# A fused attention and MLP block on one core: mixer in four groups of 112 channels, row turns and shared-key copies by DMA, w4 in the place of the q/k/v weights, and a new order

## The chip, the cores and the metric

The kernel runs on one core of one Trainium2 chip. The metric is the device time of one execution in microseconds (us); lower is better. Four engines compute: TensorE (PE, with its weight loads shown apart as PEld), VectorE (DVE), ScalarE (ACT) and GpSimd (POOL). SyncE (SP) only issues DMAs here; every DMA of the kernel is issued from SP, in SP's program order, and each engine runs its own instructions strictly in the order in which the program lists them.

## The reference

One sequence of 2048 positions with 448 channels, bf16. First a sliding local attention with 16 heads of 28 channels, in which a position sees itself and seven earlier positions two apart; then a mixer that shifts four channel groups along the sequence; then an MLP with 1792 hidden channels.

```
def _A_ref(x, wqkv, wo):
    H = 16; Dh = D // H; W, dil = 8, 2
    qkv = (x @ wqkv).reshape(B, S, 3, H, Dh)
...
    idx = pos[:, None] - off[None, :]
    mask = idx >= 0
...
    logits = jnp.einsum("bhsd,bhswd->bhsw", q, kg) * scale
    logits = jnp.where(mask[None, None, :, :], logits, -1e9)
    attn = _softmax(logits, axis=-1)
    o = jnp.einsum("bhsw,bhswd->bhsd", attn, vg)
...
def _B_ref(x, w1, w2, w3, w4):
    h = _gelu(_layernorm(x, axis=-1) @ w1)
    c = D // 4
    g0 = jnp.pad(h[:, :, 0*c:1*c], ((0, 0), (1, 0), (0, 0)))[:, :S, :]
    g1 = jnp.pad(h[:, :, 1*c:2*c], ((0, 0), (0, 1), (0, 0)))[:, 1:, :]
    g2 = jnp.pad(h[:, :, 2*c:3*c], ((0, 0), (2, 0), (0, 0)))[:, :S, :]
    g3 = jnp.pad(h[:, :, 3*c:   ], ((0, 0), (0, 2), (0, 0)))[:, 2:, :]
    hs = jnp.concatenate([g0, g1, g2, g3], axis=-1) @ w2
    x1 = x + hs
    h2 = _gelu(_layernorm(x1, axis=-1) @ w3) @ w4
    return x1 + h2
...
    h = x + _A_ref(_layernorm(x, axis=-1), A_wqkv, A_wo)
    h2 = h + _B_ref(_layernorm(h, axis=-1), B_w1, B_w2, B_w3, B_w4)
```

Here `off` is `arange(W) * dil`, and `kg` and `vg` are k and v at the positions `idx`.

## The kernel before

The sequence is cut into four blocks of 512 rows (t = 0 to 3) for attention and mixer, and into five units (u = 0 to 4) of 2, 4, 4, 4 and 2 tiles of 128 rows for what follows. A phase and its block or unit are written together: A23 is phase A2 of block 3, W30 is phase W3 of unit 0, T0 is phase T of unit 0.

Phases of a block. N1: layer norm of the input (written "N12" for block 2). A1: the normalized rows are turned so that channels lie on partitions, and q and k are formed; the last 64 channels of q and k of all heads go through a pair of banks X and Y into `qT` and `kr`, the other 384 into `qT` and `kk`. The keys of a block need the last 16 positions of the block before; these shared keys are copied between `kk[t]` and `kk[t+1]`, and between the halves of `kr` (lines 707 to 711), by ACT. V: the values, and SP's DMAs that lay them out in `vw` for each of the eight window positions (`vwp`, `vwa`, `vwb`, `vwc`). A2: DVE multiplies q with eight shifted views of k, in four pieces c (three of 128x4096, the last, from `kr`, of 128x2048), and PE sums over the channels of each head. S: softmax, with the weighting `pb` and a turn by PE. A3: DVE spreads the weights with a mask into `bd_r`, PE multiplies with `vw`, the result is evicted to `actT`. O: the projection with wo and the residual sum. B1: layer norm of the result and a turn by DMA. M: the mixer's first matmul with GELU into `gT`.

Phases of a unit. B2: the mixer's second matmul from the shifted `gT`, DVE adds the residual. T: layer norm and a turn by DMA. W3: the first MLP matmul with GELU into `h3T`. B3: the second one, from which DVE makes the output tiles in a ring of NO buffers that SP stores.

K and N of a matmul of 448 channels are cut into pieces with 64 rows: the helper `duo` (line 459) runs an upper and a lower half of the array side by side on two outputs, first one way round and then the other. Line 482, `sums`, deals the seven 64-channel pieces to them.

In the mixer before, `w1_s` has 512 columns: the 448 channels are put in another sequence and 64 of them appear twice, so that M makes four full groups of 128 columns. Where a group holds channels with different shifts, a second GELU writes part of its rows to another place (`MOVED`, lines 846 to 852). The 448 channels then stand in seven halves of 64 rows, and B2 needs seven matmuls for a tile; a pair of tiles takes 14.

A turn is done by PE (letter 't' in `TURN`: 32 small transposes into PSUM and two evictions for a block) or by one DMA transpose ('d'). Normalization and eviction may be given to ACT or DVE; `OTHER` lists those that leave their first engine, among them two of the four `pb` weightings, which GpSimd makes.

The order is written out by hand: every operation has a number in the sequence in which the phases create it, and `ORDER` lists all 891 numbers. Each engine runs its share of that list; the waits follow from what an operation reads and writes and from when its buffer comes free (`arrange`, line 192). All loads stand in one sequence on SP: x and the q/k/v weights first, then wo, w1 in six pieces, w2 in five, w3, w4. The arena holds w3, the q/k/v weights and w4 side by side.

Of the kernel before, what the change touches and what calls it, by code (L numbers as in the profile page):

```python
# [5 lines left out]
ACT = mybir.ActivationFunctionType  # L6
# [43 lines left out]
"""  # L50
OTHER = """
104 127 196 197 199 402 408 411 519 525 528 582 583
# [79 lines left out]
class _Sched:  # L132
# [59 lines left out]
    def arrange(self, sequence, other=()):  # L192
# [4 lines left out]
        done = set()  # L197
        self.gorder = []
        for n, k in enumerate(sequence):
# [3 lines left out]
            op.deps |= op.sdeps  # L203
            for d in op.deps | op.odeps:
                if d not in done:
                    raise RuntimeError("operation %d (%s) stands before %d (%s)" % (k, op.tag, d.idx, d.tag))
# [68 lines left out]
def bass_sequential_preLN__sliding_local_dilated__mixer_s_mlp__prompt_kernel(  # L275
# [6 lines left out]
    NST = SEQ // 512  # L282
# [12 lines left out]
    SHIFT = {(0, 0): 1, (0, 1): -2, (1, 0): -2, (1, 1): -2, (2, 0): 2, (2, 1): -1, (3, 0): -1, (3, 1): -1}  # L295
    MOVED = {0: (64, 48, 3), 1: (96, 32, 4), 2: (64, 16, 3)}
# [4 lines left out]
    A_W4 = A_W + 4 * (1344 + 128)  # L301
    A_QG = A_W4 + NF * 448
# [6 lines left out]
    with ExitStack() as es:  # L309
# [13 lines left out]
        w1_s = sb("w1_s", [128, 4, 512], BF16)  # L323
# [3 lines left out]
        st6 = sb("st6", [128, 8, 6], F32)  # L327
        mv = sb("mv", [128, 3, NTL, 2], F32)
# [20 lines left out]
        P_h3 = _Pool("h3", lambda k: h3T[:, k, :], NF + 2)  # L349
        P_st = _Pool("st", lambda k: st6[:, k, :], 8)  # L350
# [70 lines left out]
        def load_x(i, n):  # L421
            return dma("x%d" % i, xin[:, i:i + n, :], xv[:, i:i + n, :], 128 * n * D * 2)

        def load_rows(chan, dst, src, lo, n):

            for h in range(2):
                dma("%s%s" % (chan, "ab"[h]), dst[:, 2 * h:2 * h + 2, :], src[192 * h:192 * h + 256, lo:lo + n].rearrange("(c k) n -> k c n", k=128), 256 * n * 2)
# [21 lines left out]
        w4_v = B_w4.rearrange("(f k) n -> k f n", k=128)  # L449
        for f in range(0, NF, 7):  # L450
            dma("w4%d" % f, w4_s[:, f:f + 7, :], w4_v[:, f:f + 7, :], 128 * 7 * D * 2)
        for eng in ("sp", "pool", "act"):
# [576 lines left out]
```

## Time and profile before

| | us |
|---|---|
| timed runs, lowest / median / highest (3) | 192.61 / 193.52 / 194.06 |
| profiled execution | 193.18 |
| its span, first to last instruction | 191.7 |

All instructions appear under line 987, where the list is issued, so groups are told apart by their tiles: `arena` holds weights, q, k, `gT` and residual sums, `ps` is PSUM, `lntm` normalized rows, `actT` turned rows. `ps<-w_s,arena` is B2, `ps<-actT,w_s` M, `ps<-qk_r,zc` A2's sums, `ps<-bd_r,vw` A3, `ps<-ident,lntm` the turns by PE. A group's line has its count, its busy time and the mean time of one instruction in ns. Matmul ends are modelled, and matmuls overlap. In the list of stretches, each engine's busy time within the stretch stands before its number of instructions.

The page in 40 slices, each digit the busy share in tenths, with the granted TensorE clock:

```profile
PE   6999999999999868989999999999999999999994
PEld 2584533453444333347545444455444544555672
DVE  7799999999999999899876960036988022002203
ACT  4579999999999999999594998860148004821340
POOL 3240000000004000202076000022077600000000
PEclk9999999999999999999999999999999999999999
DMA  5999791004604179480805024006100812000111
```

### The profile page before, as it was taken

What the parts mean: (1) busy time and instruction counts of PE and PEld (TensorE: products, weight loads), DVE (VectorE), ACT (ScalarE), POOL (GpSimd) and SP (SyncE); (2) the same over time, 40 slices, a digit from 0 to 9 for tenths busy, and PEclk for the clock granted to TensorE, in tenths of its full rate; (3) what the DMA queues carried; (4) which work ended last, traced back from release to release, by engine and by line L of the source; (5) the groups of instructions that cost most, each with busy time, mean ns of one, the idle gap of its engine ahead of it and who ended that gap; (6) DMA issues with size and microseconds to landing.
All of it is one profiled execution on the core that took longest, in us unless ns stands there. A gap on an engine that the chain in (4) does not pass through costs nothing.

```text
span 191.7 us, 5740 instructions
## 1 busy us (share of the span) xinstructions
PE 181.3 (95%) x2482; PEld 92.6 (48%) x2482; DVE 129.5 (68%) x229; ACT 132.9 (69%) x310; POOL 29.3 (15%) x63
## 2 busy tenths in 40 slices
PE   6999999999999868989999999999999999999994
PEld 2584533453444333347545444455444544555672
DVE  7799999999999999899876960036988022002203
ACT  4579999999999999999594998860148004821340
POOL 3240000000004000202076000022077600000000
PEclk9999999999999999999999999999999999999999
DMA  5999791004604179480805024006100812000111
GB/s 144 349 268 186 190 320 36 10 3 118 149 3 85 28 64 262 140 178 5 109 3 113 2 50 87 0 3 146 36 27 0 164 51 72 0 3 0 51 48 48
DMA packets 30272, 17.03 MB, mean 89 GB/s; under 512 B 18936, under 2 KB 29736, under 8 KB 30248
## 3 DMA queue, kind: packets, MB, share of 16 engines
q1 hardware_dynamic: 30248, 16.68, 36.7%
q8 instruction: 19, 0.31, 0.7%
q14 instruction: 5, 0.04, 0.1%
HBM read 8.04 MB, written 1.84 MB: 51 GB/s over the span
## 4 chain that ended last, share of the span: by engine, by line
PE 66%; ACT 21%; DVE 5%; DMA 2%; POOL 1%; issue 1%; SPq 1%; POOLq 0%; ACTq 0%
PE ps L987 66%; ACT arena L987 7%; ACT lntm L987 4%; ACT actT L987 2%; DMA vw<-vt 2%; ACT vt L987 2%; ACT L982 1%; DVE lntm L987 1%; DVE st L987 1%; SPq L987 1%; ACT xin L987 1%; ACT ls L987 1%; ACT L987 1%; DVE bd_r L987 1%; DVE actT L987 1%
## 5 line engine op out<-in xcount | busy, mean ns | idle before, releaser
L987 PE MATMUL ps<-actT,arena 64*128 64x256 bf16 (+1 forms) x756 | 68.8, 329 | 1.3 <-DVE arena L987 0.7
L987 ACT ACTIVATE h3T<-ps 128x512 bf16<-128x512 f32 (+1 forms) x70 | 30.3, 525 | 39.3 <-PE ps L987 39.2
L987 PEld LDWEIGHTS ps<-actT,arena 64*128 64x128 bf16 x756 | 35.5, 94 | 30.7 <-PE ps L987 2.1
L987 PE MATMUL ps<-arena,h3T 64*128 64x448 bf16 (+2 forms) x434 | 44.4, 344 | 0.0
L987 ACT ACTIVATE arena<-ps 128x512 bf16<-128x512 f32 (+10 forms) x86 | 40.1, 515 | 3.5 <-PE ps L987 2.8
L987 DVE SCALAR_TENSOR_TENSOR ost<-ps,mrs,arena 128x448 bf16<-128x448 f32 (+1 forms) x17 | 10.6, 652 | 36.4 <-PE ps L987 36.4
L987 DVE TENSOR_TENSOR qk_r<-arena 128x4096 bf16<-128x4096 bf16 (+1 forms) x16 | 32.0, 2017 | 0.7 <-PE ps L987 0.5
L987 PEld LDWEIGHTS ps<-arena,h3T 64*128 64x128 bf16 (+1 forms) x434 | 23.0, 94 | 18.7 <-issue 0.2
L987 POOL TENSOR_TENSOR arena<-arena,xin 128x448 f32<-128x448 f32 x16 | 17.2, 1091 | 45.3 <-DVE lntm L987 45.3
L987 DVE TENSOR_TENSOR bd_r<-arena,bmask 80x2048 bf16<-80x2048 bf16 x16 | 18.9, 1213 | 0.9 <-PE ps L987 0.7
L987 ACT ACTIVATE actT<-ps 128x512 bf16<-128x512 f32 (+2 forms) x21 | 14.6, 743 | 2.1 <-PE ps L987 2.1
L987 PE MATMUL ps<-wo_s,actT 64*128 64x448 bf16 x128 | 14.3, 351 | 0.6 <-DVE actT L987 0.4
L987 PE MATMUL ps<-actT,w_s 64*128 64x512 bf16 x112 | 13.3, 377 | 1.5 <-ACT rs_y L987 0.7
L987 PE MATMUL ps<-arena,actT 64*128 64x448 bf16 x112 | 12.4, 350 | 0.4 <-ACT vt L987 0.4
L987 PE MATMUL ps<-w_s,arena 64*128 64x448 bf16 x112 | 11.6, 350 | 0.9 <-ACT arena L987 0.7
L987 ACT ACTIVATE lntm<-xin,nm 128x448 bf16<-128x448 bf16 x16 | 10.5, 661 | 2.6 <-DVE nm L987 2.6
L987 DVE SCALAR_TENSOR_TENSOR arena<-xin,rs_y,ps 128x448 f32<-128x448 bf16 x16 | 10.3, 672 | 2.1 <-PE ps L987 2.0
L987 DVE TENSOR_SCALAR lntm<-arena,mv,rs_y 128x512 bf16<-128x512 f32 x14 | 10.2, 774 | 2.1 <-POOL rs_y L987 2.0
L987 POOL TENSOR_TENSOR pb<-ls,mx 128x512 bf16<-128x512 f32 x2 | 3.3, 1640 | 52.6 <-ACT mx L987 52.6
L987 DVE BATCH_NORM_STATS2 st<-xin 128x6 f32<-128x448 bf16 x16 | 9.4, 614 | 0.8 <-DMA xin<-in_A_x_dram 0.8
L987 PEld LDWEIGHTS ps<-actT,w_s 64*128 64x128 bf16 x112 | 5.2, 94 | 8.6 <-PE ps L987 1.7
L987 PEld LDWEIGHTS ps<-wo_s,actT 64*128 64x128 bf16 x128 | 5.6, 94 | 7.2 <-PE ps L987 1.4
(73 smaller groups left out, 161.9 us busy)
## 6 DMA issues: line engine op xcount, KB each, us to landing
arena<-in_B_w_dram SPq DMA_DIRECT2D x2, 896.0 KB, 6.7
out_dram<-ost SPq DMA_DIRECT2D x15, 112.0 KB, 1.8
arena<-in_B_w_dram SPq DMA_DIRECT2D x2, 784.0 KB, 5.7
vw<-vt SPq DMA_DIRECT2D x4, 320.0 KB, 4.3
vw<-vt SPq DMA_DIRECT2D x4, 256.0 KB, 4.3
arena<-in_A_wqkv_dram SPq DMA_DIRECT2D x2, 448.0 KB, 5.0
xin<-in_A_x_dram SPq DMA_DIRECT2D x2, 448.0 KB, 7.5
xin<-in_A_x_dram SPq DMA_DIRECT2D x3, 224.0 KB, 5.6
```

What stands on the lines that cost most here:

```text
L982: eng.preload_act_table_set("natural_log_exp_and_others")
L987: inst = getattr(eng, meth)(**kw)
```

## The change

The mixer's groups become the reference's own four of 112 channels: `w1_s` and `w2_s` have 448 columns and 112 rows in use, each group has one shift, the second GELUs and the clearing after them go, and B2 runs four pieces in each half (64 and 48 rows), 16 matmuls for a pair of tiles. The rows of blocks 2 and 3 are turned for A1 by DMA. The shared keys are copied by DMAs of 16-element runs on SP, four in blocks 0 to 2 and two in block 3. w4 is put where the q/k/v weights lie and loaded after V3. All four `pb` weightings are on DVE. The output ring has five buffers, the loads of w1 and w2 are one of two pieces and one of one. ORDER is new, with 858 numbers; on SP it has the sequence x and q/k/v weights; block 0's shared keys; the turn of A12; V0's value copies mixed with block 1's keys; the turn of A13; wo; V1's copies; further keys, w1 and the turn of B10; w2 and the turn of B11; w3; the turn of T0; V3's copies and w4; the turn of B12. Other engines' shares change with it: on PE, W30 begins before A23's last two sums and the second half of B21; after M3 comes one group of B31 and then B23; on DVE, A23's last two products and two residual adds of O2 stand behind T0's normalizations, two evictions of A32 and one more normalization of B10 go to ACT, and T1's normalizations stand ahead of A33's last masks.

`HALO = 'dddd'` selects the key DMAs. `STAGE = '....'` and `ALONE = False` leave their branches unused.

```
-TURN = {'A1': 'tttt', 'B1': 'dddd', 'B2': 'ddddd'}
+TURN = {'A1': 'ttdd', 'B1': 'dddd', 'B2': 'ddddd'}
-NBD, NLN, NACT, NSM, NO = 3, 2, 4, 1, 3
+NBD, NLN, NACT, NSM, NO = 3, 2, 4, 1, 5
+HALO = 'dddd'
+STAGE = '....'
+ALONE = False
 ORDER = """
...
-    SHIFT = {(0, 0): 1, (0, 1): -2, (1, 0): -2, (1, 1): -2, (2, 0): 2, (2, 1): -1, (3, 0): -1, (3, 1): -1}
-    MOVED = {0: (64, 48, 3), 1: (96, 32, 4), 2: (64, 16, 3)}
+    SHIFT = (-1, 1, -2, 2)
+    GC = D // 4
...
-    A_W4 = A_W + 4 * (1344 + 128)
-    A_QG = A_W4 + NF * 448
+    A_W4 = A_W
+    A_QG = A_W4 + max(NF * 448, 4 * (1344 + 128))
...
-        for k, (to, lo, n) in enumerate(((0, 112, 336), (336, 0, 112), (448, 48, 64))):
-            load_rows("w1%d" % k, w1_s[:, :, to:to + n], B_w1, lo, n)
-        dma("w2", w2_s[:, 0:2, :], B_w2[112:368, :].rearrange("(c k) n -> k c n", k=128), 256 * D * 2)
-        for k, (lo, c, src, n) in enumerate(((0, 2, 368, 80), (80, 2, 0, 48), (0, 3, 48, 64), (64, 3, 48, 64))):
-            dma("w2%d" % k, w2_s[lo:lo + n, c, :], B_w2[src:src + n, :], n * D * 2)
+        load_rows("w1", w1_s, B_w1, 0, D)
+        dma("w2", w2_s[0:GC, :, :], B_w2.rearrange("(c k) n -> k c n", k=GC), D * D * 2)
...
+            if HALO[t] == "d":
...
+                    end = lambda h, lo, n: kr[t][64 * h:64 * h + 64, lo:lo + n, 64:]
+                dma("kra%d" % t, kr[t][64:128, :, 0:PADK], end(0, 0, 4), 64 * 4 * PADK * 2)
+                dma("krb%d" % t, kr[t][0:64, 1:4, 0:PADK], end(1, 0, 3), 64 * 3 * PADK * 2)
+                if t + 1 < NST:
+                    dma("krc%d" % t, kr[t + 1][0:64, 0:1, 0:PADK], end(1, 3, 1), 64 * PADK * 2)
+                    dma("kkc%d" % t, kk[t + 1][:, :, 0:PADK], kk[t][:, :, 512:KVW], 128 * 3 * PADK * 2)
+            else:
...
-            S.add("dve", "tensor_tensor", alts=[("pool", [("tensor_tensor", mult)])], **mult)
+            dve("tensor_tensor", **mult)
...
             def group(g, upper):
                 b = _Tile(P_bank)
-                def evict():
-                    act(gT[:, g, 2 + t * 512:2 + (t + 1) * 512], b(), ACT.Gelu_apprx_tanh)
-                    if g in MOVED:
...
+                return sums(lambda lo, n: b(halves(lambda v: v[0:GC, lo:lo + n], n // 128)), lambda c, part: w1_s[part, c, g * GC:(g + 1) * GC],
+                            lambda c, part, lo, n: rows(a, c, lo // 128, n // 128, part), upper), \
+                    lambda: act(gT[0:GC, g, 2 + t * 512:2 + (t + 1) * 512], b(lambda v: v[0:GC, :]), ACT.Gelu_apprx_tanh)
...
+        def load_w4():
+            last = S.ops[-1]
+            w4_v = B_w4.rearrange("(f k) n -> k f n", k=128)
+            for f in range(0, NF, 7):
+                dma("w4%d" % f, w4_s[:, f:f + 7, :], w4_v[:, f:f + 7, :], 128 * 7 * D * 2).odeps.add(last)
...
-                return (lambda lo, n: b(lambda v: v[:, lo:lo + n]), side(0, 3 + upper), side(1, 4 - upper)), out
+                return (lambda lo, n: b(lambda v: v[:, lo:lo + n]), side(TOP), side(slice(64, GC))), out
...
+                    if S.tag == "V%d" % (NST - 1):
+                        S.tag = "w4"
+                        load_w4()
```

More of the change, by code (lines that the diff above doesn't have):

```diff
@@ L197, in arrange @@
         done = set()
+        turned, moved = [], []
         self.gorder = []
@@ L203, in arrange @@
             op.deps |= op.sdeps
+            if not ALONE:
+                pass
+            elif op.insts[0][0] == "dma_start_transpose":
+                op.deps.update(turned + moved)
+                turned, moved = [op], []
+            elif op.is_dma and not callable(op.chan):
+                op.deps.update(turned)
+                moved.append(op)
             for d in op.deps | op.odeps:
@@ L442, in bass_sequential_preLN__sliding_local_dilated__mixer_s_mlp__prompt_kernel @@
             dma("wo%d" % j, wo_s[32 * j:32 * j + DH, :, :], wo_v[j], DH * D * 8)
[L443 to L455 removed]
+        load_rows("w1", w1_s, B_w1, 0, D)
+        dma("w2", w2_s[0:GC, :, :], B_w2.rearrange("(c k) n -> k c n", k=GC), D * D * 2)
+        load_rows("w3", w3_s, B_w3, 0, F)
+        loads = [op for op in S.ops if op.is_dma]
+        for a, b in zip(loads, loads[1:]):
+            b.odeps.add(a)
         TOP, BOT = slice(0, 64), slice(64, 128)
@@ L703, in phase_A1 @@
             duo(half(X, 0, True), half(Y, 64, False), ((0, 256),))
-            for h, b in enumerate((X, Y)):
-                copy(qT[64 * h:64 * h + 64, 3, now:now + 256], b(lambda v: v[0:64, 0:256]))
-                copy(kr[t][64 * h:64 * h + 64, :, PADK:], b(lambda v: v[64:128, 0:256].rearrange("p (j n) -> p j n", j=4)), False)
-            copy(kr[t][64:128, :, 0:PADK], last(X, 0, 4), False)
-            copy(kr[t][0:64, 1:4, 0:PADK], last(Y, 0, 3), False)
-            if t + 1 < NST:
-                copy(kr[t + 1][0:64, 0:1, 0:PADK], last(Y, 3, 1), False)
-                copy(kk[t + 1][:, :, 0:PADK], kk[t][:, :, 512:KVW])
+            if STAGE[t] == "d":
+                stage = _Tile(P_sg)
+                for h, b in enumerate((X, Y)):
+                    copy(stage(lambda v, h=h: v[:, h, :]), b(lambda v: v[:, 0:256]))
+                for h in range(2):
+                    dma("sq%d%d" % (t, h), qT[64 * h:64 * h + 64, 3, now:now + 256], stage(lambda v, h=h: v[0:64, h, :]), 64 * 512)
+                    dma("sk%d%d" % (t, h), kr[t][64 * h:64 * h + 64, :, PADK:], stage(lambda v, h=h: v[64:128, h, :].rearrange("p (j n) -> p j n", j=4)), 64 * 512)
+            else:
+                for h, b in enumerate((X, Y)):
+                    copy(qT[64 * h:64 * h + 64, 3, now:now + 256], b(lambda v: v[0:64, 0:256]))
+                    copy(kr[t][64 * h:64 * h + 64, :, PADK:], b(lambda v: v[64:128, 0:256].rearrange("p (j n) -> p j n", j=4)), False)
@@ new lines, in phase_A1 @@
+            if HALO[t] == "d":
+                if STAGE[t] == "d":
+                    end = lambda h, lo, n: stage(lambda v: v[64:128, h, :].rearrange("p (j n) -> p j n", j=4)[:, lo:lo + n, 64 - PADK:])
+                else:
+                    end = lambda h, lo, n: kr[t][64 * h:64 * h + 64, lo:lo + n, 64:]
[4 more added lines that the diff above has]
+                    dma("kkc%d" % t, kk[t + 1][:, :, 0:PADK], kk[t][:, :, 512:KVW], 128 * 3 * PADK * 2)
+            else:
+                copy(kr[t][64:128, :, 0:PADK], last(X, 0, 4), False)
+                copy(kr[t][0:64, 1:4, 0:PADK], last(Y, 0, 3), False)
+                if t + 1 < NST:
+                    copy(kr[t + 1][0:64, 0:1, 0:PADK], last(Y, 3, 1), False)
+                    copy(kk[t + 1][:, :, 0:PADK], kk[t][:, :, 512:KVW])
@@ L718, in group @@
                 b = _Tile(P_bank)
-                return sums(lambda lo, n: b(lambda v: v[:, 0:D]), lambda c, part: a(lambda v: v[part, il, c, :]),
-                            lambda c, part, lo, n: wqkv_s[part, c, 2 * D:3 * D], upper), \
+                return sums(lambda lo, n: b(lambda v: v[:, lo:lo + n]), lambda c, part: a(lambda v: v[part, il, c, :]),
+                            lambda c, part, lo, n: wqkv_s[part, c, 2 * D + lo:2 * D + lo + n], upper), \
                     lambda: copy(vt[:, sl, il, :].rearrange("p (h n) -> p h n", n=32)[:, :, 0:DH], b(lambda v: v[:, 0:D].rearrange("p (h n) -> p h n", n=DH)))
@@ L868, in phase_B2, with group, side @@
             summed = STATS["B2"][u] == "a"
-            def group(i, upper):
+            def group(i):
                 b = _Tile(P_bank)
-                def side(h, n):
-                    part = (TOP, BOT)[h]
-                    return [(gT[part, c, 2 + i * 128 + SHIFT[c, h]:130 + i * 128 + SHIFT[c, h]], (lambda lo, m, c=c: w2_s[part, c, lo:lo + m])) for c in range(n)]
+                def side(part):
+                    return [(gT[part, c, 2 + i * 128 + SHIFT[c]:130 + i * 128 + SHIFT[c]], (lambda lo, m, c=c: w2_s[part, c, lo:lo + m])) for c in range(4)]
                 def out():
@@ L910, in group @@
                 b = _Tile(P_bank)
-                return sums(lambda lo, m: b(halves(lambda v: v[:, 0:128 * n], n)), lambda c, part: w3_s[part, c, f * 128:(f + 1) * 128],
-                            lambda c, part, lo, m: rows(a, c, 0, n, part), upper), \
+                return sums(lambda lo, m: b(halves(lambda v: v[:, lo:lo + m], m // 128)), lambda c, part: w3_s[part, c, f * 128:(f + 1) * 128],
+                            lambda c, part, lo, m: rows(a, c, lo // 128, m // 128, part), upper), \
                     lambda: act(h3[u][f](lambda v: v[:, 0:128 * n]), b(lambda v: v[:, 0:128 * n]), ACT.Gelu_apprx_tanh)
```

27 lines of the change are left out of this document (9 added, 18 removed), and 59 rows, old and new, of the table ORDER.

## Prediction

> **What bounds the kernel now.** I read the page first, then busy time by stretches, then the chain of waits and the timeline around the point where the chain changes engine. The profiled execution took 193.18 us, 191.7 of them span; the three timed runs have the median 193.52. I make the sum against 193.18.
>
> ```profile
> PE 181.3 (95%) x2482; PEld 92.6 (48%) x2482; DVE 129.5 (68%) x229; ACT 132.9 (69%) x310; POOL 29.3 (15%) x63
> ```
>
> ```profile
> core 0: us, PE busy (x) PEld busy (x) DVE busy (x) ACT busy (x) POOL busy (x), PEclk, DMA share, GB/s
> 13.00:50.00 37.00, 36.39 (x610) 17.16 (x608) 36.76 (x43) 36.72 (x96) 0.00 (x0) 1.00 0.54 128
> 50.00:84.00 34.00, 30.40 (x544) 13.23 (x542) 32.92 (x57) 33.30 (x77) 3.53 (x3) 1.00 0.47 105
> 84.00:100.40 16.40, 15.17 (x316) 9.14 (x310) 14.43 (x27) 14.18 (x35) 4.43 (x6) 1.00 0.36 61
> 100.40:188.20 87.80, 87.79 (x909) 45.94 (x910) 34.01 (x75) 41.82 (x86) 16.07 (x18) 1.00 0.20 47
> ```
>
> ```profile
> 100.41 87.81 PE ps L987 x907
> ```
>
> The 95% hides two regimes. From 13 to 84 us VectorE (DVE) and ScalarE (ACT) are both busy nearly all the time; of 71 us DVE idles 1.3 and ACT 1.0. TensorE (PE) loses 3.6 us in the second stretch and 1.2 us in the third. From 100.4 to 188.2 PE is busy for 87.79 of 87.80 us, the chain of waits has it as one piece of 907 matmuls, and the other two engines have slack. So the end is the moment at which PE's unbroken run begins plus the work left for it. What the change does to ACT is worth something only as far as DVE lets it through, and what it does to the late stage only as far as it adds or removes matmuls.
>
> ```profile
> 79.69 1.00 DVE L987 TENSOR_SCALAR lntm<-arena,nm,rs_y 128x512 bf16<-128x512 f32 x2
> 80.72 1.26 SPq L987 DMA_TRANSPOSE actT<-lntm  x1
> 84.07 1.04 PE L987 MATMUL ps<-actT,arena 64*128 64x256 bf16 x16
> 85.82 2.38 PE L987 MATMUL ps<-actT,arena 64*128 64x256 bf16 x36 [0.71 <-DVE arena L987]
> ```
>
> This is the hand-over: DVE ends T0's two normalizations at 80.69, they are turned by DMA, and W30, the first filler with much PE work, starts at 84.07. Two operations of 0.54 us take 1.00 here: on DVE each starts 0.08 us before its predecessor ends.
>
> **Matmuls.** The mixer's output sum (B2) goes from seven to eight row-pair steps in each of eight pairs of tiles, so 16 matmuls are added. Two blocks of A1 turns leave PE, 64 of the 96.
>
> ```profile
> L987 PE MATMUL ps<-w_s,arena 64*128 64x448 bf16 x42 | 4.1, 349 | 0.0
> ```
>
> ```profile
> L987 PE MATMUL ps<-ident,lntm 64*128 64x64 bf16 x96 | 2.1, 191 | 0.0
> ```
>
> The first row is a stretch (130.2 to 134.3) with PE full: 21 pairs in 4.1 us, 0.195 each, so eight pairs add 1.6 us. The second gives 64/96 of 2.1, 1.4 us less. Net +0.2 us, and the removed part lies where PE had idle time anyway.
>
> **ScalarE.** The change takes off it four evictions of turned rows, twelve repeated GELUs (three per block) and fourteen key copies.
>
> ```profile
> L987 ACT ACTIVATE actT<-ps 128x512 bf16<-128x512 f32 x12 | 6.8, 615 | 2.1 <-PE ps L987 2.1
> L987 ACT ACTIVATE actT<-ps 128x1024 bf16<-128x1024 bf16 x6 | 6.2, 1077 | 0.0
> ...
> L987 ACT ACTIVATE arena<-ps 48x512 bf16<-48x512 f32 x3 | 1.8, 587 | 0.1
> ...
> L987 ACT ACTIVATE arena<-ps 64x64 bf16<-64x64 f32 x4 | 0.9, 216 | 0.1
> ...
> L987 ACT ACTIVATE lntm<-xin,nmr,rs_y 128x512 bf16<-128x512 bf16 x1 | 0.8, 803 | 0.0
> ```
>
> That is 4 x 1.08 + 12 x 0.59 + 14 x 0.22 = 14.5 us. Back come two evictions of A32 (2 x 0.62), and one normalization of B10 (0.80): about 12.4 us of relief in all, most of it ahead of T0. The switches between ACT's function tables are as many in the new order as in the old. ACT therefore stops binding, and DVE remains.
>
> **VectorE.** I counted in the two printed orders what stands in front of T0's last normalization on DVE.
>
> ```profile
> L987 DVE TENSOR_TENSOR qk_r<-arena 128x4096 bf16<-128x4096 bf16 x12 | 27.3, 2283 | 0.2 <-ACT arena L987 0.2
> ...
> L987 DVE TENSOR_TENSOR qk_r<-arena 128x2048 bf16<-128x2048 bf16 x4 | 4.9, 1218 | 0.5 <-PE ps L987 0.5
> L987 DVE SCALAR_TENSOR_TENSOR xin<-ps,xin 128x448 bf16<-128x448 f32 x8 | 4.7, 622 | 1.8 <-PE ps L987 1.5
> ...
> L987 DVE TENSOR_SCALAR lntm<-xin,nm,rs_y 128x512 bf16<-128x512 bf16 x11 | 3.9, 396 | 0.0
> ...
> L987 DVE CAST actT<-ps 128x512 bf16<-128x512 f32 x4 | 2.7, 682 | 0.0
> ...
> L987 DVE TENSOR_TENSOR pb<-ls,mx 128x512 bf16<-128x512 f32 x2 | 1.4, 683 | 0.0
> ```
>
> ```profile
> L987 POOL TENSOR_TENSOR pb<-ls,mx 128x512 bf16<-128x512 f32 x2 | 3.3, 1640 | 52.6 <-ACT mx L987 52.6
> ```
>
> Gone from in front of it: two products of A23 (2.28 and 1.22), two A32 evictions (1.36), two residual adds of O2 (1.24) and one normalization of B10 (0.40), 6.5 us. New in front of it: the weighting of block 2, which GpSimd did in 1.64 us (0.68), and one eviction of A10 (priced as the CAST, 0.68), 1.37 us; two smaller copies trade places. Net 5.1 us, less 0.08 for each of six fewer operations: 4.7 us earlier, if DVE stays gapless. Over the whole attention part the two DVE lists are equal within half a microsecond, so there is nothing else to win on DVE.
>
> Not all of the 4.7 arrives. The new order leaves one product (2.28) between B20's adds and T0's scale, and in that time ACT must square two tiles, take two small functions and a table load.
>
> ```profile
> L987 ACT ACTIVATE lntm<-xin,nm 128x448 bf16<-128x448 bf16 x16 | 10.5, 661 | 2.6 <-DVE nm L987 2.6
> ...
> L987 ACT ACT_TABLE_LOAD x6 | 7.7, 1283 | 0.1
> ```
>
> 2 x 0.66 + 1.28 + about 1 for the accumulator reads and small functions is 3.6, so DVE waits about 1.3 us. The bounds are 0 and 1.3, and I take 1.3. T0 then ends 3.4 us earlier and W30 could start at 80.7.
>
> **What PE has done by then.** The new order also puts less in front of W30: 1.4 us of transposes, two of A23's sums (12 of its 112 column-packed matmuls), and 12 of the 28 matmuls of B21 (six pairs, 1.2 us) fewer, minus 0.2 for the eighth step in B20: about 2.9 us with 0.6 for A23. So PE stands 3.4 - 2.9 = 0.5 us better at W30. From there to 100.4 the old order lost another 1.2 us (16.40 - 15.17), partly to a PSUM bank that DVE freed late (the 0.71 above). With DVE 3 to 4 us ahead I expect that loss to go; it may stay whole, since A33's last masks come four microseconds later in DVE's list, behind T1's normalizations. Gain 0.5 to 1.7, I take 1.7.
>
> **DMA and its queue.** SP gets two more turns, fourteen key copies, and the weights in another order.
>
> ```profile
> arena<-in_B_w_dram SPq DMA_DIRECT2D x2, 896.0 KB, 6.7
> out_dram<-ost SPq DMA_DIRECT2D x15, 112.0 KB, 1.8
> arena<-in_B_w_dram SPq DMA_DIRECT2D x2, 784.0 KB, 5.7
> ...
> actT<-lntm SPq DMA_TRANSPOSE x9, 4.3
> out_dram<-ost SPq DMA_DIRECT2D x2, 56.0 KB, 1.6
> ...
> vw<-vt SPq DMA_DIRECT2D x3, 16.0 KB, 4.8
> ```
>
> A key copy is not in this trace. Its bounds are 1.6 us (a small store into an idle queue) and 6.7 (behind a weight load); the nearest row is the 16 KB copy with many rows, 4.8. On ACT it took 0.22. Waiting for each block's copies are DVE's last product of A2 and, on SP behind them, block 2's turn and V0's value copies. In the new order two further DVE products, some 4.5 us, mostly stand between the key eviction and that last product, and w1, w2, wo and w3 no longer fill the queue before 35 us, so I cost it at nothing; uncovered it would be up to 6.7 - 2.3 per block. The turns of A12 and A13 (4.3) have to be back before PE reaches A12; N12's normalizations stand at nearly the same place of DVE's list as before, and the new PE order puts about 5 us more work in front of A12, so nothing. w4 can now start only after V3's matmuls and stands on SP behind T0's turn and three value copies: from the end of the turn's issue about 2.5 us for those, 1.2 for its own two issues and 5.7 to land, 9.4 in all. B30 wants it 2.1 us (84.07 - 81.98) plus W30's 49 pairs at 0.12 (x36 in 2.38), B21's other eight pairs (1.6) and A23's two sums (0.6) later, about 10.2. Slack 0.8, price 0 to 1.5, I take 0.2; B12's turn waits behind w4 on SP, but DVE needs longer than that to normalize it. The larger output ring and the fewer loads of w1 and w2 change nothing in a stage where only PE binds.
>
> After M3 the new order has one group of 14 matmuls (seven pairs, 1.4 us) before B23 needs M3's GELUs, where the old one had seven such groups. The last two GELUs take 2 x 0.6, behind ACT's evictions of W31: price 0 to 1.2, I take 0.2.
>
> **Sum.** 193.18 - 1.7 + 0.2 (matmuls) + 0.2 (w4) + 0.2 (M3) = 192.1; I say 192.0. With every bound on the good side it is -3.0 (1.7 and T0's 1.3) + 0.2, 190.4; on the bad side -0.5 + 0.2 + 1.5 + 1.2, 195.6.
>
> **A rule against the change.** M's weights shrink from 128 to 112 columns.
>
> ```profile
> L987 PE MATMUL ps<-actT,w_s 64*128 64x512 bf16 x112 | 13.3, 377 | 1.5 <-ACT rs_y L987 0.7 <-ACT rs_x L987 0.7
> ...
> L987 PEld LDWEIGHTS ps<-actT,w_s 64*128 64x128 bf16 x112 | 5.2, 94 | 8.6 <-PE ps L987 1.7 <-ACT rs_x L987 1.1 <-ACT rs_y L987 0.8
> ...
> L987 PEld LDWEIGHTS ps<-ident,pb 64*80 64x80 bf16 x64 | 1.7, 117 | 0.9 <-issue 0.3 <-ACT arena L987 0.3
> ```
>
> An 80-column load takes longer than a 128-column one here, 117 against 94 ns. Scaled by columns, 112 would take 164. Loads of the two halves overlap (112 x 94 ns in 5.2 us), and the pair of 512-column matmuls beside them takes 13.3/56 = 0.24 us, so I cost it at nothing. The Trainium skill, page "TensorE: Matmul & The Clock Gate", section "Weight-path perf modes", says that the fast weight load is on only with 128 weights; the trace agrees with its direction. On its figures the loss would be about a factor of two on a load, and still hidden.
>
> **Rivals.** *Keys late (slower).* If a key copy lands after 4.8 us with only one product (2.28) as cover, DVE idles 2.5 us in that block, and DVE has no slack before 84. It decides once the landing exceeds the cover. In one block that gives 192.0 + 2.5 = 194.5, in two 197.0; I take 196. Against it speak the emptier queue and the gapless order. Beside it stands the page "DMA: Bandwidth & Descriptors", section "Specifications", of the Trainium skill: pieces under 512 B are read, modified and written. The copied runs are 32 B; no row here isolates such a copy. *Turns hold the queue (slower).* V0's value copies now stand behind A12's turn, which waits for DVE; a late block 0 costs up to one landing, 4.3, less what PE does meanwhile: about 195.5. *Exposed weight loads.* If the 70 ns (164 - 94) show in each of M's 56 pairs, 3.9 us: 195.9. *No net change.* T0's gain is spent on waits at A33, w4 or M3: 193.2, within 0.9. *All of it arrives.* ACT keeps up at T0 and DVE's order gives 3 us: 190.4.
>
> **Chances.** Forecast as summed (190.8 to 192.9) 0.40, all arrives 0.08, no net change 0.20, keys late 0.17, turns 0.10, weight loads 0.05. About 1%, 1.9 us, is what a measurement tells from no change. Below 191.6: 0.08 and 0.26 of the forecast's 0.40, 0.34. Above 195.4: the three slower cases and a rest, 0.34. Between: 0.32. The range 189.9 to 196.6 leaves out two blocks of late keys and worse, and a gain beyond 3 us. Of the likeliest case alone the range is 190.8 to 192.9.
>
> **What would show it.** Right: ACT has visible idle between 13 and 84 and DVE none; W30 begins near 80.7; PE runs unbroken from 99 or earlier; 32 small transposes are left; B2 has 128 matmuls. Wrong: DVE waiting for a DMA before a product of A2, matmuls of A3 waiting for the value copies, B30 waiting for w4, B23 for a GELU, or M's pairs spaced wider than now.

## The result, and the profile after

The changed kernel takes 191.68 us (median of 10 runs, 190.94 to 192.49), the kernel before 193.43 in the same sitting (10 runs, 192.61 to 194.26). The ratio is 0.9905 with a 95% interval of 0.9886 to 0.9925: 1.75 us, or 0.95%, faster. The profiled execution took 191.99 us, 190.3 of them span; before it was 193.18 and 191.7. The ratios compare fast runs, and where two of a kernel's six runs lay over 1.5% above its fastest (the old mixer, the first try in the old order), its time below is the median of the other four.

The first line is the page's busy time of the changed kernel; the next four are its busy time by the same stretches as before (us, then PE, PEld, DVE, ACT, POOL, granted clock, DMA share, GB/s).

```profile
PE 180.0 (95%) x2434; PEld 96.3 (51%) x2434; DVE 129.9 (68%) x226; ACT 123.4 (65%) x282; POOL 26.5 (14%) x61
```

```profile
13.00:50.00 37.00, 35.08 (x549) 17.46 (x544) 36.28 (x44) 35.05 (x90) 0.00 (x0) 1.00 0.43 88
50.00:84.00 34.00, 32.82 (x596) 16.61 (x594) 33.66 (x55) 33.08 (x78) 0.73 (x1) 1.00 0.70 172
84.00:100.40 16.40, 15.71 (x308) 9.20 (x302) 14.85 (x28) 11.69 (x24) 2.49 (x4) 1.00 0.51 116
100.40:188.20 87.80, 86.58 (x890) 46.16 (x886) 34.32 (x72) 38.27 (x80) 18.04 (x19) 1.00 0.17 41
```

ACT lost 9.5 us of work and now idles 2.9 of the 71 us between 13 and 84; DVE still idles only 1.1. PE's idle time in the second stretch fell from 3.60 to 1.18 us. Two of the four stretches got worse: the first (0.61 to 1.92) and, above all, the last, which was gapless and now has 1.22 us of gaps. Ahead of 13 us, where nothing is listed, PE's idle time went from 2.12 to 3.24 us.

The hand-over of T0, from the timeline (start, duration; the releaser stands in brackets where there was a wait):

```profile
71.97 2.29 DVE L1011 TENSOR_TENSOR qk_r<-arena 128x4096 bf16<-128x4096 bf16 x1
74.17 0.15 DVE L1011 TENSOR_TENSOR nmr<-nm,rs_y 128x2 f32<-128x2 f32 x1
74.36 1.00 DVE L1011 TENSOR_SCALAR lntm<-arena,nm,rs_y 128x512 bf16<-128x512 f32 x2
...
75.40 1.25 SPq L1011 DMA_TRANSPOSE actT<-lntm  x1
...
77.11 1.93 PE L1011 MATMUL ps<-w_s,arena 64*128 64x448 bf16 x16
78.88 1.36 PE L1011 MATMUL ps<-actT,arena 64*128 64x256 bf16 x22
```

T0's normalizations end at 75.37 instead of 80.69, with no gap on DVE between the product and T0's scale: the root from ACT was ready at 74.08. The turn lands at 78.50, and W30 starts at 78.88 (84.07 before) straight behind B21's matmuls, without a stop of PE. What PE does wait for is in its list of waits (us in total, times, longest), with the one long wait of DVE's list below, and the late pieces of the chain:

```profile
PE ps L1011 <- DMA wo_s<-in_A_wo_dram: 1.0, 1, 1.0
...
PE ps L1011 <- ACT h3T L1011: 0.4, 1, 0.4
PE ps L1011 <- DVE arena L1011: 0.3, 1, 0.3
...
DVE lntm L1011 <- ACT rs_y L1011: 11.7, 1, 11.7
```

```profile
111.05 7.90 PE ps L1011 x70
...
127.75 59.27 PE ps L1011 x623
```

Where one piece of 87.8 us ran from 100.41 to 188.22, PE now stops at 111.05 for a GELU's buffer and at 127.75 for a bank, and ends at 187.02. Counting every matmul ahead of a point at the same pair spacing (an estimate), PE had lost 13.7 us when it reached O3 before and 11.0 after (2.7 better), 13.9 and 12.05 at M3, 14.8 and 13.5 at the last sum of B34. So the change won about 2.7 us up to 100 us and gave 1.4 of it back.

### The profile page after: what moved, and what is told of

It is laid out like the page before. It is cut to its first block, busy times and chain, and to the rows that moved or that the text cites. A ratio compares the mean times of both kernels' runs of the same rounds, so it can differ in the third digit from the quotient of the medians.

```text
span 190.3 us, 5623 instructions
## 1 busy us (share of the span) xinstructions
PE 180.0 (95%) x2434; PEld 96.3 (51%) x2434; DVE 129.9 (68%) x226; ACT 123.4 (65%) x282; POOL 26.5 (14%) x61
## 4 chain that ended last, share of the span: by engine, by line
PE 56%; DVE 22%; ACT 11%; DMA 5%; SPq 2%; issue 2%; DVEq 0%; ACTq 0%
PE ps L1011 56%; DVE qk_r L1011 6%; DVE lntm L1011 5%; DVE bd_r L1011 4%; DMA arena<-in_A_wqkv_dram 3%; ACT lntm L1011 3%; SPq L1011 2%; DMA wo_s<-in_A_wo_dram 2%; ACT arena L1011 2%; DVE arena L1011 1%; ACT xin L1011 1%; DVE mx L1011 1%; DVE st L1011 1%; ACT h3T L1011 1%; ACT rs_x L1011 1%
## 5 line engine op out<-in xcount | busy, mean ns | idle before, releaser
L1011 PE MATMUL ps<-actT,arena 64*128 64x512 bf16 (+1 forms) x756 | 69.4, 329 | 0.9 <-ACT h3T L1011 0.4
L1011 PEld LDWEIGHTS ps<-actT,arena 64*128 64x128 bf16 x756 | 37.3, 94 | 28.5 <-PE ps L1011 2.1
L1011 ACT ACTIVATE arena<-ps 128x512 bf16<-128x512 f32 (+3 forms) x63 | 31.5, 541 | 3.7 <-PE ps L1011 3.2
L1011 DVE TENSOR_TENSOR bd_r<-arena,bmask 80x2048 bf16<-80x2048 bf16 x16 | 19.8, 1270 | 0.1
L1011 POOL TENSOR_TENSOR arena<-arena,xin 128x448 f32<-128x448 f32 x16 | 17.1, 1086 | 14.8 <-DVE lntm L1011 14.8
L1011 DVE TENSOR_SCALAR lntm<-arena,mv,rs_y 128x512 bf16<-128x512 f32 x14 | 8.9, 679 | 12.2 <-ACT rs_y L1011 11.7
L1011 PE MATMUL ps<-wo_s,actT 64*128 64x448 bf16 x128 | 14.8, 350 | 1.1 <-DMA wo_s<-in_A_wo_dram 1.0
L1011 PE MATMUL ps<-w_s,arena 64*128 64x448 bf16 (+1 forms) x128 | 14.2, 350 | 0.1
L1011 PE MATMUL ps<-actT,w_s 64*112 64x512 bf16 x112 | 13.4, 378 | 0.0
L1011 ACT ACTIVATE actT<-ps 128x512 bf16<-128x512 f32 (+2 forms) x18 | 11.2, 653 | 3.2 <-PE ps L1011 3.2
L1011 POOL TENSOR_TENSOR mrs<-nm,rs_y 128x4 f32<-128x4 f32 x4 | 1.5, 387 | 71.9 <-ACT rs_y L1011 70.1
L1011 PEld LDWEIGHTS ps<-actT,w_s 64*112 64x112 bf16 x112 | 7.0, 127 | 4.7 <-DMA actT<-lntm 0.4
```

The source lines that it names most:

```text
L1011: inst = getattr(eng, meth)(**kw)
```

## The experiments

Each was timed against the kernel before; ratios have 95% intervals. Profiles of kernels whose lists are the same up to 63 us differ there by up to 0.7 us (A3's late sums begin at 66.81 to 67.47 us), so a difference between two profiles is read together with what it was ahead of the edit.

**T0 later, by 3.5 us of products.** In `ORDER`, T0's scale and normalizations (548, 549, 550) go behind A23's last two products (482, 484); what those need goes with them.

```
-478 548 549 550 399 400 403
+478 27 28 353 479 481 482 484 548 549 550 399 400 403
```

> The changed kernel with T0's scale, two normalizations and turn moved behind A23's last two products in VectorE's list (2.28 + 1.22 = 3.5 us); no operation is added or taken away. Theory H (the gain is T0's earlier hand-over): W30 starts near 82.4 us instead of 78.9, PE loses some 3 us more ahead of it, of which the late run gives back part; 1.5 to 2.5 us slower than the changed kernel, 193.2 to 194.2, ratio to the kernel before 0.998 to 1.004. Rival L (W30's start has slack and the late run sets the time): not more than 0.3 us slower, at most 192.0, ratio up to 0.993.

198.97 us, ratio 1.0277 (1.0242 to 1.0312): 7.3 us slower than the changed kernel, where 1.5 to 2.5 were expected. W30 started at 84.15. The wait of PE, a wait of DVE that the edit made, and busy time by stretches (the column ahead of the last two is the granted clock):

```profile
PE ps L1011 <- DMA actT<-lntm: 5.5, 1, 5.5
```

```profile
76.45 3.43 DVE L1011 TENSOR_TENSOR qk_r<-arena 128x4096 bf16<-128x4096 bf16 x2 [2.54 <-PE ps L1011]
```

```profile
78.00:82.00 4.00, 0.69 (x8) 0.16 (x4) 3.96 (x10) 0.00 (x0) 0.00 (x0) 1.00 0.00 0
82.00:83.00 1.00, 0.00 (x0) 0.00 (x0) 1.00 (x5) 0.00 (x0) 0.00 (x0) 0.73 0.81 161
83.00:88.00 5.00, 3.85 (x36) 2.24 (x40) 0.91 (x4) 4.00 (x12) 0.00 (x0) 0.50 0.82 194
88.00:90.00 2.00, 2.00 (x22) 0.74 (x16) 1.20 (x2) 1.80 (x4) 0.00 (x0) 0.68 1.09 379
```

The two products, moved ahead, first had to wait 2.54 us for PE to free their buffer, so that T0 ended 5.6 us later (80.98 against 75.37) and not 3.5. PE stood still for 5.5 us, its clock fell to half and came back only after 88 us: PE was busy for 5.85 us between 83 and 90 at a mean near 0.55, which is 2.6 us of work lost. A23's last sums stand behind W30 in PE's list, so DVE then waited 4.8 us for S3. Rival L is out. The sign is H's; the price was not one for one.

**T0 later, by 2.5 us of adds.** Now only behind O2's adds (399, 400, 403, 404).

```
-478 548 549 550 399 400 403 404 405
+478 399 400 403 404 548 549 550 405
```

> The changed kernel with T0's scale, two normalizations and turn behind O2's four adds (4 x 0.62 = 2.5 us) in VectorE's list; nothing else moves. The larger move cost 7.3 us, of which PE's clock at 0.50 after 5.5 us of idle explains some 2.5. Theory H (each microsecond that T0 is late delays PE's unbroken run by about one): W30 starts near 81.4 us, the clock stays at 1.00 since it only fell 3.7 us after PE's last matmul, 2.0 to 3.0 us slower than the changed kernel, 193.7 to 194.7, ratio to the kernel before 1.001 to 1.007. Rival L (W30 has slack): at most 192.1, ratio up to 0.994. Rival D (A23's sums, which stand behind W30 on PE, make VectorE idle too, so that the cost is over-proportional): above 195, ratio over 1.009.

193.46 us, ratio 1.0012 (0.9989 to 1.0035): the whole gain is gone, and the clock stays at 1.00 in the profiled execution.

```profile
PE ps L1011 <- DMA actT<-lntm: 2.0, 1, 2.0
```

W30 started at 80.39, 1.5 us later than in the changed kernel, and the span grew by 1.3 (191.6 against 190.3). But this profile was 0.66 us ahead before the edit bears (A3's late sums at 66.81 instead of 67.47), so the edit's own delay is about 2.2 us: the adds, 2.5, less the 0.4 that the turn had to spare. In the medians it cost 1.8. As long as the clock holds, a microsecond of T0 is nearly a microsecond of the end. H holds, a little under its price of 2.0 to 3.0 us.

**The old mixer in the new order.** `w1`, `w2`, M and B2 are those of the kernel before, repeated GELUs and all; the rest is the changed kernel.

```
-    SHIFT = (-1, 1, -2, 2)
-    GC = D // 4
+    SHIFT = {(0, 0): 1, (0, 1): -2, (1, 0): -2, (1, 1): -2, (2, 0): 2, (2, 1): -1, (3, 0): -1, (3, 1): -1}
+    MOVED = {0: (64, 48, 3), 1: (96, 32, 4), 2: (64, 16, 3)}
...
+                        act(gT[lo:lo + m, g, at + skip:at + 512], b(lambda v: v[lo:lo + m, skip:]), ACT.Gelu_apprx_tanh)
```

> The changed kernel with the mixer of the kernel before in the new order: 128-channel groups, twelve repeated GELUs of 0.59 us back on ScalarE (three of them ahead of T0's small functions), 16 matmuls of B2 fewer on PE (1.6 us, 1.4 of them late). Theory H (ScalarE idles 2.9 us between 13 and 84 us in the changed kernel, which covers the 1.8 us ahead of T0): W30 starts at most 1 us later, and PE has less work: 190.3 to 191.7, ratio to the kernel before 0.983 to 0.991. Rival A (the gain comes from ScalarE's relief by the mixer): W30 2 to 3 us later, 192.5 to 193.7, ratio 0.995 to 1.001.

199.39 us (200.22 over all six), ratio 1.0316 (1.0264 to 1.0369). Both expectations missed. The waits for GELUs, and the stretches around the first long one:

```profile
PE ps L1025 <- ACT arena L1025: 7.5, 5, 2.3
```

```profile
66.00:68.00 2.00, 0.42 (x32) 0.32 (x32) 2.00 (x3) 1.91 (x4) 0.00 (x0) 1.00 1.53 150
68.00:70.00 2.00, 0.80 (x6) 0.43 (x8) 1.79 (x1) 1.98 (x5) 0.00 (x0) 0.59 0.78 206
70.00:74.00 4.00, 4.00 (x54) 1.58 (x52) 1.29 (x4) 3.37 (x6) 0.00 (x0) 0.50 1.02 402
```

In the new order B20 stands directly behind M0, so M0's GELUs and their repeats are on PE's path: B20 waited 2.2 us for the last of them, the clock fell, and B21, B22 and B23 had waits of the same kind behind M1, M2 and M3 (0.8, 1.5 and 2.3 us), at which the clock stayed at 1.00. The expectation had counted what ACT has to do ahead of T0, not who stands directly behind it. ACT's relief by the mixer is a condition of the new order, though ACT idles only 2.9 us with it.

**The key copies back on ACT.** `HALO = '....'`, with the fourteen copies right behind the key evictions; in `ORDER` their numbers move there.

```
-HALO = 'dddd'
+HALO = '....'
```

> The changed kernel with the fourteen key copies back on ScalarE, right behind the key evictions (0.22 us each, 3.1 us in all, 2.6 of them ahead of 50 us); nothing else moves. Theory S (ScalarE has no room to give back: the old mixer's three repeated GELUs of M0 held B20 for 2.2 us): ScalarE ends its work ahead of T0 later, W30 starts 0.3 to 1.0 us later, 192.0 to 192.8, ratio to the kernel before 0.992 to 0.997. Rival D (the copies by DMA are themselves what someone waits for, so that their price was not nothing): 0.3 us faster or more, at most 191.4, ratio up to 0.990.

193.49 us, ratio 1.000 (0.9981 to 1.0019). Rival D is out; S has the sign and W30's delay (79.88, 1.0 us later), but too small a price: 0.3 to 1.1 us expected, 1.8 measured. DVE's normalizations now wait for ACT's roots three times instead of once:

```profile
DVE lntm L1011 <- ACT rs_y L1011: 13.0, 3, 11.7
```

The span grew by 0.9 us in the profiled execution (191.2 against 190.3), but by 1.5 in the median of all runs (191.5 against 189.95). The other 0.3 us lies outside the span (2.0 against 1.7 in the median), and nothing in the trace explains it.

**The parts in the old order.** All parts of the change, with the lists of PE, DVE, ACT and GpSimd as before. It was tried three times, with SP's list sorted in three ways.

> All parts of the change in the order of the kernel before: mixer in four groups, turns of A12 and A13 by DMA right behind their last normalization, key copies by DMA right behind the key evictions, w4 in the place of wqkv behind V3; block 2's and 3's weighting stays on GpSimd. Theory H (the new order, by its earlier T0, makes the gain; ScalarE's relief by itself is worth little because VectorE's list is as long as before): T0's last normalization ends near 80 us (it was 80.7), the time is 192.8 to 193.6, ratio to the kernel before 0.996 to 1.001. Rival A (the relief of ScalarE makes the gain): 191.5 to 192.2, ratio 0.989 to 0.993. Rival K (DMAs that the old order leaves no time for): above 194, ratio over 1.003.

209.60 us (210.46 over all six), ratio 1.0842 (1.0795 to 1.0889): the last x load stood on SP behind the first key copies, landed at 19.6 us, and PE stood still for 7.1 us.

> All parts of the change with the lists of PE, VectorE, ScalarE and GpSimd as in the kernel before (what is left out of them apart); SP's list is sorted by the time at which each transfer was ready in the trace of before, the x loads ahead of the first key copies, which the first try of this had the other way round. Theory H (the new order, by its earlier T0, makes the gain): T0's last normalization ends at 79.5 to 81, PE is busy from there as before, 192.6 to 193.7, ratio to the kernel before 0.995 to 1.001. Rival A (the relief of ScalarE makes the gain): 191.2 to 192.2, ratio 0.988 to 0.993. Rival K (transfers that the old order leaves no time for): above 194, ratio over 1.003.

202.96 us, ratio 1.0506 (1.048 to 1.0532): up to 64 us no stop of PE exceeded 1.8 us, but block 1's turn stood behind w3 and w4, and its issue held SP for 9.64 us.

```profile
66.13 3.82 SPq L1011 DMA_DIRECT2D arena<-in_B_w_dram  x4
70.00 9.64 SPq L1011 DMA_TRANSPOSE actT<-lntm  x1
```

> As the last try with the lists of the kernel before, with one mend on SP: there w3 and w4 stood ahead of block 1's turn, whose issue then took 9.6 us; here w3 stands behind that turn and w4 behind T0's. Theory H (the new order, by its earlier T0, makes the gain, and the parts by themselves nothing): T0's last normalization ends at 79.5 to 81, 192.6 to 193.7, ratio to the kernel before 0.995 to 1.001. Rival A (the relief of ScalarE makes the gain in any order): 191.2 to 192.2, ratio 0.988 to 0.993. Rival K (another transfer is late in the old lists): above 194, ratio over 1.003.

195.98 us, ratio 1.0127 (1.0101 to 1.0153). T0's last normalization ended at 83.26, 2.57 us after that of the kernel before, and DVE has one stop ahead of it, of that size:

```profile
81.12 1.23 DVE L1011 TENSOR_TENSOR qk_r<-arena 128x2048 bf16<-128x2048 bf16 x1 [2.57 <-PE ps L1011]
```

The view names PE, whose last matmul ended at 80.40. But the sums that free this product's buffer had ended at 77.92 (in the kernel before, in the same order, at 78.50, and the product began at 78.55), and the trace holds DVE's wait for the semaphore of block 3's key copy, from 76.14 to 81.07. That copy, issued behind w3 at 73.2, landed at 81.04: it set the start. Without this stop T0 would have ended at 80.69 (83.26 - 2.57, an estimate), where the kernel before has it and H expected it. PE stopped for 2.0 us there, and its clock fell to 0.50. All three runs ended as K, none at H's time: the parts need SP's list sorted anew, and in none of my three sortings did ACT's relief alone win anything. Whether some sorting makes the old order equal to the kernel before stays open; A has no support.

**T2's root on DVE and GpSimd.** One letter:

```
-POWER = {'N1': 'aaaa', 'B1': 'aaaa', 'B2': 'apapp'}
+POWER = {'N1': 'aaaa', 'B1': 'aaaa', 'B2': 'apppp'}
```

> The changed kernel with T2's reciprocal root computed by VectorE and GpSimd, where ScalarE's Ln and Exp were (one letter; the places in the order stay). In the changed kernel VectorE waited 11.7 us for that Exp at 123.3 us, and the adds of B23 and B24 behind it freed their banks late. Theory G (about 0.6 of the 1.2 us that PE gives back in the late run come from this wait): the wait shrinks below 3 us, PE's stop ahead of W32 (0.3 us at 127.75) goes, 0.3 to 0.7 us faster than the changed kernel, 191.0 to 191.4, ratio to the kernel before 0.985 to 0.989. Rival N (PE only loses it at the next wait, for a GELU or a bank): within 0.2 us of 191.7, ratio 0.989 to 0.992.

190.25 us, ratio 0.9828 (0.980 to 0.9857): 1.4 us better than the changed kernel, where 0.3 to 0.7 were expected. Both late stops are gone, and PE runs in one piece again, to 185.49:

```profile
96.94 88.55 PE ps L1011 x967
```

Only the stop at 127.75 was T2's. The other came from GpSimd: the new root stands ahead of T1's third add in GpSimd's list, so that add no longer runs beside B13's mean on DVE. The next run moves the add alone.

**One GpSimd add later.** T1's third add (614) goes behind B13's product of mean and root (525); T2's root stays on ACT.

```
-745 807 614 647 653 654 648 525 612 613
+745 807 647 653 654 648 525 614 612 613
```

> The changed kernel with one GpSimd operation moved: T1's third add of 128x448 stands behind B13's product of mean and root, so that it no longer runs at 104.2 to 105.3 us. In the changed kernel VectorE's small operation for B13's mean took 0.94 us there, in the run with T2's root on GpSimd 0.17, and B13's squares began 0.8 us earlier. Theory C (GpSimd's add and VectorE's operation hold each other up): that operation takes under 0.3 us, PE's stop of 0.40 us at 111 goes, 0.4 to 0.9 us faster than the changed kernel, 190.8 to 191.3, ratio to the kernel before 0.984 to 0.989; VectorE's wait of 11.7 us at T2 and PE's stop ahead of W32 stay. Rival N (the 0.94 is chance): within 0.2 us of 191.7, ratio 0.989 to 0.992.

191.62 us, ratio 0.990 (0.9879 to 0.992), as N said of the time; at B13 the mechanism is C's. B13's mean in the changed kernel, with GpSimd's adds beside it, and then in this one:

```profile
102.24 3.02 POOL L1011 TENSOR_TENSOR arena<-arena,xin 128x448 f32<-128x448 f32 x3
...
104.34 0.94 DVE L1011 TENSOR_SCALAR nm<-mv 128x4 f32<-128x4 f32 x1
```

```profile
101.93 2.03 POOL L1011 TENSOR_TENSOR arena<-arena,xin 128x448 f32<-128x448 f32 x2
...
104.03 0.17 DVE L1011 TENSOR_SCALAR nm<-mv 128x4 f32<-128x4 f32 x1
```

The stop at 111 is gone and M3 starts 1.0 us earlier (0.3 of it was there ahead of the edit). Then PE waits 1.03 us instead of 0.29 ahead of the last piece, which begins at 127.48.

T2's root on ACT came 1.0 us earlier too, but the add now runs beside T2's normalizations on DVE, which became longer. The changed kernel, and then this run:

```profile
123.11 2.21 POOL L1011 TENSOR_TENSOR arena<-arena,xin 128x448 f32<-128x448 f32 x2
...
123.34 3.17 DVE L1011 TENSOR_SCALAR lntm<-arena,mv,rs_y 128x512 bf16<-128x512 f32 x4 [11.71 <-ACT rs_y L1011]
```

```profile
122.11 3.39 POOL L1011 TENSOR_TENSOR arena<-arena,xin 128x448 f32<-128x448 f32 x3
...
122.34 3.90 DVE L1011 TENSOR_SCALAR lntm<-arena,mv,rs_y 128x512 bf16<-128x512 f32 x4 [11.57 <-ACT rs_y L1011]
```

So 0.73 of the 1.0 us won at B13 was lost again at T2, and the adds of B23 behind those normalizations freed PE's bank only 0.3 us earlier. The edit moved the price of the GpSimd add and did not remove it; what the add would cost at a place with nothing beside it is not shown. With T2's root on GpSimd the normalizations begin at 112.06, with one add beside them, and take 2.62 us.

**wo's loads ahead of block 3's turn.**

```
-152 237 259 153
+152 237 20 21 22 23 259 153
...
-454 455 20 240 21 22 23 251
+454 455 240 251
```

> The changed kernel with one edit: the four loads of wo stand on SP ahead of block 3's turn instead of behind it. In the changed kernel O0's first matmuls waited 1.0 us for wo at 44.1 us. Theory H (VectorE's hand-over of T0 sets when W30 starts, and PE's losses ahead of it are covered): the wait for wo goes, W30 still starts behind T0's turn near 78.9 us, the time stays within 0.3 us of the changed kernel's 191.7 (ratio to the kernel before 0.989 to 0.992). Rival P (PE's lost microseconds ahead of 79 us add up to the end): 1.0 us less, about 190.7, ratio 0.985 to 0.987.

191.15 us, ratio 0.9877 (0.9851 to 0.9904), which overlaps the changed kernel's interval; the median, 0.5 us faster, lies between H's bound (191.4) and P's 190.7. In the trace the wait for wo is gone, W30 starts at 78.15, and the last piece, as long as before, 0.9 us earlier, of which 0.4 was there ahead of the edit (PE at 35.28 instead of 35.70): it begins at 126.84.

P has the direction. In neither kernel does W30 wait for T0's turn, and on DVE a wait of 0.34 us at 49.89, for O0's result from ACT, is gone too; its T0 ends 1.0 us earlier, about half of it by the edit.

**Both edits together.**

> The changed kernel with both edits: wo's loads ahead of block 3's turn, and T2's reciprocal root on VectorE and GpSimd. Theory P (PE's lost microseconds add up to the end): the two gains of 0.5 and 1.4 us add, 189.4 to 190.0, ratio to the kernel before 0.979 to 0.983; PE starts B34 near 180.0 us. Rival E (one eats the other, since a later wait takes what the first frees): 190.1 to 190.5, ratio 0.983 to 0.986.

189.73 us, ratio 0.9815 (0.9792 to 0.9839): P.

**And T0's adds moved on GpSimd.** 552 and 551 go behind T0's last normalization (550), beside O2's adds on DVE.

```
-478 548 549 550 399 400
+478 548 549 550 552 551 399 400
```

> The two edits together (189.73), and T0's two adds on GpSimd moved from the stretch of A33's masks, where two masks took 3.2 us instead of 2.4, to right behind T0's normalizations, where VectorE has O2's four adds. Theory C: A33's first two masks take 2.4 us together, A33 and O3 come up to 0.8 us earlier, PE's stop at A33 (0.5) goes: 189.0 to 189.5, ratio to the kernel before 0.977 to 0.980. Rival M (the adds hold up O2's adds or A23's product instead): 189.6 to 190.5, ratio 0.981 to 0.985.

189.46 us, ratio 0.9786 (0.9765 to 0.9807), 2.1% faster than the kernel before. A33's first two masks, in the run before this one and in this one, and this one's longest piece of the chain:

```profile
91.36 3.19 DVE L1011 TENSOR_TENSOR bd_r<-arena,bmask 80x2048 bf16<-80x2048 bf16 x2
```

```profile
91.70 2.36 DVE L1011 TENSOR_TENSOR bd_r<-arena,bmask 80x2048 bf16<-80x2048 bf16 x2
```

```profile
89.24 95.23 PE ps L1011 x1103
```

The masks became 0.83 us shorter, PE's stop at A33 is gone, and PE runs in one piece from 89.24 on; the time falls into C's range, but the interval overlaps that of the two edits alone. This is the fastest version found, clearly ahead of both kernels.

## Why the prediction was right

The forecast was 192.0 and the median is 191.68; the sum was made against the profiled 193.18, and the profiled execution after took 191.99. The two 1.2s agree by luck, because errors in the terms cancelled: up to 100 us the sum had 1.7 and the trace shows 2.7, and behind that the sum gave back 0.6 (matmuls, w4, M3) and the trace 1.4.

- *The bound.* That PE's unbroken run starts when T0's hand-over lets it was right: some 2.2 us more at W30 cost 1.8, the whole gain. That DVE then remains the only bound was half right: at W30 the turn has 0.4 us to spare, and a wait of PE for wo 35 us earlier shows in the end.
- *Matmuls, +0.2.* B2 has 128 matmuls and 32 small transposes of the kind before are left, as said. The net size can't be read: PE's busy time fell by 1.3 us, but rows that interleave overlap, and their ends are modelled.
- *ACT's relief, 12.4 us, "ACT therefore stops binding".* Page: 132.9 to 123.4, 9.5. It has 2.9 us of idle time to 84 us, but no room: 3.1 us of key copies put back cost the whole gain, and the mixer's repeats cost 7.7 us, the fallen clock included.
- *"DVE waits about 1.3 us" for T0's squares.* This step failed. ACT was ready 0.2 us ahead of DVE, so the lower bound, 0, was the right one. The 3.6 us counted a table load of 1.28 between B20's adds and the root; in the new order it stands ahead of the squares, at 69.57, and squares, accumulator reads and small functions took 1.98 us, from 72.10 to 74.08:

```profile
69.57 1.28 ACT L1006 ACT_TABLE_LOAD   x1
...
73.88 0.20 ACT L1011 ACTIVATE rs_y<-rs_x 128x2 f32<-128x2 f32 x1
```

With 5.3 us earlier instead of the 4.7 of the list, W30 came at 78.88 and not 80.7.
- *A gain of 0.5 to 1.7 up to 100 us.* Mis-sized, for the same reason: PE stood 2.7 us better at O3. (The work that leaves PE ahead of W30 adds up to 3.0, not 2.9: 1.4 + 0.6 + 1.2 - 0.2.) About 0.5 us more would have come without the wait for wo, by the run with wo's loads ahead; the forecast did not see that wait: it counted the emptier queue ahead of 35 us as a gain and not what O0 at 44 us needs.
- *Key copies at nothing, w4 0.2, M3 to B23 0.2.* None of the three waits occurred. The copies land after 2.1 to 3.2 us in the median:

```profile
arena<-arena SPq DMA_DIRECT2D x4, 8.0 KB, 3.2
arena<-arena SPq DMA_DIRECT2D x4, 6.0 KB, 2.5
arena<-arena SPq DMA_DIRECT2D x3, 12.0 KB, 2.1
```

One behind w3 takes 6.94, and its product starts 4.7 us after it landed. The late keys of the rival did occur in the old order: behind w3 a copy took 7.83 us, and DVE stood still for 2.57. *Turns hold the queue* did not occur either: block 2's turn was issued at 21.6 us, and no matmul of A3 waited for the value copies behind it.
- *The late run, gapless.* This step failed: "Gain 0.5 to 1.7" was carried to the end, less only w4's 0.2 and M3's 0.2, and of the signs named, "PE runs unbroken from 99 or earlier" did not show. About 1.4 us were given back, at B13's mean and at T2's late root and normalizations, with GpSimd's adds beside both. "No net change" had the mechanism, at other places (A33, w4, M3) than the real ones.
- *Exposed weight loads.* The rival did not occur:

```profile
L1011 PE MATMUL ps<-actT,w_s 64*112 64x512 bf16 x112 | 13.4, 378 | 0.0
...
L1011 PEld LDWEIGHTS ps<-actT,w_s 64*112 64x112 bf16 x112 | 7.0, 127 | 4.7 <-DMA actT<-lntm 0.4 <-ACT h3T L1011 0.3
```

A 112-column load takes 127 ns, not the 164 scaled from 80 columns, against 94 for 128; M's matmuls take 13.4 us as before. For the rule of the Trainium skill, page "TensorE: Matmul & The Clock Gate", section "Weight-path perf modes", the sign holds, the factor of two does not show here, and the cost was nothing.

## What to carry to other kernels

Moving work off a nearly full engine paid here through the order that it allows: the parts in the old lists were 1% to 8% slower, and the new order with the old mixer 3% slower. When a hand-over comes earlier, read on to the end for the next operation that stands behind a slow small one; here a one-letter move of T2's root was worth almost as much as the whole change. An operation moved out of the way still costs where it lands: the GpSimd add taken from beside B13's mean lengthened T2's normalizations instead, and the time stayed the same.

## What the runs showed of the hardware

After some pauses PE's clock fell to half and stayed there for 6.83 us (T0 behind the products, old mixer) or 3.41 (third old-order try), so that such a pause cost more than its length: 5.5 us of standing still cost 2.6 us of work besides. 2.2 us (with 0.42 us of small matmuls in the 2 us around its start) was enough in the run with the old mixer, where the clock fell some 1.3 us after the last matmul (0.59 in the mean from 68 to 70 us), and 2.0 us in the third old-order try. Yet a pause of 2.3 us ahead of B23, in the same run with the old mixer, left it at 1.00, and so did 2.0 us in the profiled run with T0 behind O2's adds; of that kernel's twelve runs two, at 194.84 and 195.04 us, have a mean clock of 0.991. The length of the pause alone does not decide. The kernel before shows it too: of 45 runs beside the experiments 23 have a mean granted clock of 0.982 to 0.991 (median 193.78 us) and 22 one of 0.998 to 1.00 (193.19), while the changed kernel's ten all have 0.999 or 1.00; so some 0.2 of the 1.75 us (193.43 - 193.19, an estimate across sittings) may be clock that the old order lost, at a place that its profile, with 1.00 throughout, does not show. The Trainium skill, page "TensorE: Matmul & The Clock Gate", section "Part 1: The HAM clock gate", puts the fall after an idle window of about 3.4 us that runs freely; the half rate and the stays of 3.41 and 6.83 us agree, but here pauses shorter than one window were enough, sometimes.

Beside a GpSimd add of 128x448, which takes 1.03 us, a small DVE operation took 0.94 us instead of 0.17, two masks 3.2 instead of 2.36, and T2's four normalizations 3.90 with three adds instead of 3.17 with two, while O2's adds, which read PSUM, kept their 0.62. The Trainium skill, page "SBUF — State Buffer", section "SBUF: two separate sides", says that the port pair these engines share is locked for a whole instruction; the 0.7 to 0.8 us lost to each add, most of its length, agree with that.

A DMA turn behind the four loads of w3 and w4 held SP's queue for 9.64 us; in that run the issue of the other ten took 1.2 to 3.7 us.
